# Three modulation vectors move from TensorE to VectorE, their weights turned by DMA, in a one-core transformer block

## The chip, the core and the metric

The kernel runs on one core of a Trainium2 chip. The metric is the device time of one execution in microseconds (us). A core has TensorE (matmuls, into PSUM), VectorE, ScalarE and GpSimd (POOL in the profile), each with an instruction queue of its own that it works through in order, and the SP engine, whose queue only issues DMA transfers here. POOL issues some transfers too. Engines wait for each other through semaphores; the scheduler of the kernel language sets those from the tiles that instructions read and write.

## The reference, cut to what matters

```python
mod = (silu(c) @ w_mod).reshape(1, 6, 1, 1024)          # c: [1, 1024], w_mod: [1024, 6*1024]
sa, ca, ga, sb, cb, gb = mod[:, 0] ... mod[:, 5]
h = layernorm(x) * (1 + ca) + sa                        # x: [1, 2048, 1024]
# linear attention, 32 heads of 32:
q, k, v = split(h @ wqkv);  phi(t) = where(t > 0, t + 1, exp(t)) + 1e-6
kv = einsum('bhsd,bhse->bhde', phi(k), v);  z = phi(k) summed over s
o = (phi(q) @ kv) / (phi(q) . z + 1e-6)
x = x + ga * (o @ wo)
h = layernorm(x) * (1 + cb) + sb
x = x + gb * ((silu(h @ w_gate) * (h @ w_up)) @ w_down) # w_gate, w_up: [1024, 3584]
```

All inputs are bf16. Each of the six modulation vectors is a product of one row, silu(c), with a 1024 x 1024 block of w_mod.

## The kernel before

The 2048 tokens are worked in four chunks of 512 (`sc` = 0 to 3), each of four tiles of 128. For each chunk the kernel computes phi(k) (`k_phase`, eight groups of eight 128x512 matmuls), adds the chunk before to the sum kv (`kv_phase`), and computes v (`v_phase`, eight groups). While v is computed, VectorE and ScalarE normalise the next chunk (`ln1`), a DMA transpose on the SP queue turns it to features by tokens (`hT`), and VectorE applies 1 + ca and sa (`modulate_all`). A phi group (`phi_to`) takes an exponential on ScalarE and two instructions on VectorE (L290, L292) before its PSUM buffer is free; `acc_a` has four such buffers, `acc_b` another four. V groups are evacuated by ScalarE alone.

phi(q) of chunk 0 follows its v; the Q groups of chunks 1 to 3 come after the last kv, as filling between small steps that wait for one another: `KVB` and `Zden` (VectorE, from the finished sum `kv_acc`), two TensorE transposes into `tpk` and their copy `KVT`, the sums of the denominator of chunk 0 (`den_sum(0)`), its reciprocal and its way through DRAM to a broadcast layout (`den_spread`), and four folds (`fold_wo`), which multiply kv into the output weight wo, so that attention and output projection become one product (`wo_tile`, matmul group a_ps). The four PSUM banks of a fold are emptied by ScalarE and VectorE, two each. Then come the second LayerNorm and the feed-forward part (`gate_up`, `down`), from about 210 us to the end.

The vectors sa and ca are computed at the start from `wma` and `wmb`; fillers (`keep_warm`, products of zeros) keep TensorE busy there. gb is summed on VectorE later (`gb_sum`, L366 and L368). The three others are made on TensorE: `ga_rows` in chunk 2 and `mod_rows` in chunk 3, between the fourth and the fifth K group, 32 narrow matmuls each into the tile `modr`, from blocks `wml` of w_mod that `mod_load` fetches on SP. The rows go through DRAM on the POOL queue: ga comes back as a broadcast `ga_bc`, sb and cb as columns `sbT` and `cb1T`. VectorE multiplies wo by `ga_bc` (L553) before the folds. Large tiles share one pool of 19 buffers (`big`).

TensorE's order is that of the program (`mm` keeps it). The order of the other engines is the scheduler's, except in the opening block `in_order` and where `tc.issue_after` names an instruction to follow. SP's queue is in order, so a transfer that waits for its buffer holds those behind it.

Of the kernel before, what the change touches and what calls it, by code (L numbers as in the profile page):

```python
# [15 lines left out]
LN_EPS = 1e-5  # L16
# [5 lines left out]
def kernel(  # L22
# [86 lines left out]
    def acc_b(name, shape=(NB,), dt=F32):  # L109
        return pb.tile([P] + list(shape), dt, name=name, tag="pb")  # L110
# [4 lines left out]

    x_tiles = {}

    def load_x(st, eng):
        x_sb = k2.tile([P, D], BF16, name="x_sb")
        eng.dma_start(out=x_sb[:], in_=x2[st * P:(st + 1) * P, :])  # L120
        x_tiles[st] = x_sb
# [64 lines left out]
    sa0T, ca0T = scr[:, :, 0, 0], scr[:, :, 1, 0]  # L186
    sbT = const.tile([P, DC], F32, name="sbT")
    cb1T = const.tile([P, DC], F32, name="cb1T")
    ga_t = ep.tile([P, NB], F32, name="e")
    ga_bc = ga_t[:].bitcast(BF16)  # L190
# [10 lines left out]
    def build_masks():  # L201
        nc.gpsimd.memset(zmask[:], 0.0)
        for h in range(HPC):
            rs = slice(h * DH, (h + 1) * DH)
            for hg in range(HG):
                nc.gpsimd.memset(zmask[rs, hg, HG * h + hg:HG * h + hg + 1], 1.0)

    def rstd_of(mv, n):
        veps = small.tile([P, STC], F32, name="veps")
        nc.vector.tensor_scalar_add(out=veps[:, 0:n], in0=mv[:, 0:n, 1], scalar1=LN_EPS)  # L210
        rstd = small.tile([P, STC], F32, name="rstd")
        nc.gpsimd.tensor_tensor(out=rstd[:, 0:n], in0=veps[:, 0:n], in1=neg_half[:].to_broadcast([P, n]), op=ALU.pow)  # L212
        return rstd
# [10 lines left out]
    def normalise_act(dst, src, mv, rstd):  # L224
        nmr = small.tile([P, 1], F32, name="nmr")
        nc.gpsimd.tensor_scalar(out=nmr[:], in0=mv[:, 0, 0:1], scalar1=rstd[:, 0:1], scalar2=-1.0,  # L226
                                op0=ALU.mult, op1=ALU.mult)
        nc.scalar.activation(out=dst, in_=src, func=ACT.Identity, bias=nmr[:], scale=rstd[:, 0:1])  # L228
# [20 lines left out]
    def ln1_norm(sc, t, x_sb, mv, rstd, dve=False):  # L249
        xn = k2.tile([P, D], BF16, name="xn", bufs=4)  # L250
        if dve:
            normalise(xn[:], x_sb[:], mv[:, 0, 0:1], rstd[:, 0:1])
        else:
            normalise_act(xn[:], x_sb[:], mv, rstd)
        if sc > 0:
            nc.sync.dma_start_transpose(hTs[sc][:, :, t * P:(t + 1) * P], xn[:])
        return xn
# [50 lines left out]
    def k_phase(sc, lo, hi):  # L308
        if lo == 0:
            pks[sc] = big("pk", [STC, D])  # L310
        for g in k_groups[lo:hi]:
            accs = [acc_a()]
            k_mms(sc, [g], accs)
            k_evac(sc, [g], accs)

    def v_phase(sc):
# [11 lines left out]

    def q_phase(sc, lo=0, hi=DC):
        if lo == 0:  # L330
            pqs[sc] = big("pq", [HG, SCW])
        for qc in range(lo, hi):
            acc = acc_a()
            for cc in range(DC):
                mm(acc[:], lhsT=wq[cc // 4][:, cc % 4, qc * P:(qc + 1) * P], rhs=hTs[sc][:, cc, :],
                                 start=(cc == 0), stop=(cc == DC - 1))
            phi_to(pqs[sc][:, qc, :], acc[:])

    def v_ones(v, lo):
# [3 lines left out]
    def kv_phase(sc):  # L343
# [7 lines left out]
        if sc == 0:  # L351
            nc.vector.tensor_copy(out=kv_acc, in_=kvv)
        else:
            nc.vector.tensor_tensor(out=kv_acc, in0=kv_acc, in1=kvv, op=ALU.add)

# [13 lines left out]

    def ga_rows(blks):  # L370
        ps = acc_b("modr")
        H2 = NB // 2
        for j in range(DC):
            for g in range(4):
                mm(ps[32 * g:32 * g + 32, 0:H2], lhsT=sc32[:, j, :], rhs=blks[g // 2][:, j, (g % 2) * H2:(g % 2 + 1) * H2],
                   start=(j == 0), stop=(j == DC - 1))
        row = small.tile([P, NB], BF16, name="mrow", bufs=1)
        nc.scalar.copy(out=row[:, 0:H2], in_=ps[:, 0:H2])
        for g in range(4):
            nc.gpsimd.dma_start(out=mrow_dram[0, g:g + 1, 0:H2], in_=row[32 * g:32 * g + 1, 0:H2])  # L380
        nc.gpsimd.dma_start(out=ga_bc.rearrange("p (g n) -> p g n", g=4),
                            in_=mrow_dram[0, :, 0:H2].unsqueeze(0).to_broadcast([P, 4, H2]))

    gb_rows = []

    def mod_load(cols):
        blks = []
        for lo in cols:
            t = big("wml", [DC, NB])
            nc.sync.dma_start(out=t[:], in_=wm_v[:, :, lo:lo + NB])  # L390
            blks.append(t)
        return blks

    def mod_rows(blks):
        ps = acc_b("modr")
        for j in range(DC):
            for g in range(4):
                mm(ps[32 * g:32 * g + 32, :], lhsT=sc32[:, j, :], rhs=blks[g][:, j, :],
                                 start=(j == 0), stop=(j == DC - 1))
        row = small.tile([P, NB], BF16, name="mrow", bufs=1)  # L400
        nc.scalar.copy(out=row[:], in_=ps[:])
        return row

    mrow_dram = dram.tile([2, 4, NB], BF16, name="mrow_scratch")

    def mod_spread(k, row):
        for g in range(4):
            nc.gpsimd.dma_start(out=mrow_dram[k, g:g + 1, :], in_=row[32 * g:32 * g + 1, :])
        cols = small.tile([P, 2 * DC], BF16, name="mcol", bufs=1)
        with nc.allow_non_contiguous_dma(reason="2048 elements, once"):  # L410
            nc.gpsimd.dma_start(out=cols[:], in_=mrow_dram[1].rearrange("g (i p) -> p (g i)", p=P))
        nc.vector.tensor_copy(out=sbT[:], in_=cols[:, 0:DC])
        nc.vector.tensor_scalar_add(out=cb1T[:], in0=cols[:, DC:2 * DC], scalar1=1.0)

# [9 lines left out]

    def den_sum(sc):
        pq = pqs[sc]
        den = acc_b("den")
        for hg in range(HG):
# [28 lines left out]
    def keep_warm(acc, n):  # L457
        for _ in range(n):
            mm(acc[:], lhsT=sel[:, 0, :], rhs=sel[:], start=True, stop=True)

    gs = k_groups[0:6]
    accs = [acc_a() if i < 4 else acc_b("acc") for i in range(6)]
    spare = accs[5]
    keep_warm(spare, 9)
    hT = hTs[0] = big("hT", [DC, SCW])
    pks[0] = big("pk", [STC, D])
    H = 3 * P
    with in_order(nc.vector, nc.scalar, nc.gpsimd):
# [8 lines left out]
        xns = [ln1_norm(*st0)] + [ln1_norm(*ln1_stats(0, t)) for t in range(1, 3)]  # L477
        keep_warm(spare, 6)
        mod_rows_a(0)
        pe_transpose_tile(hT, xns[0], 0)  # L480
        keep_warm(spare, 3)
        mod_rows_a(1)
# [31 lines left out]
    with tc.issue_after(last_on[nc.gpsimd.engine]):  # L514
        build_masks()
        nc.gpsimd.tensor_copy(out=scf[:], in_=scT[:])

    for sc in range(NSC):
        if sc > 0:
            k_phase(sc, 0, 2)  # L520
            kv_phase(sc - 1)
            k_phase(sc, 2, 4)
            if sc == 2:
                ga_rows(blks)
            if sc == 3:
                mod_spread(1, mod_rows(blks))
            k_phase(sc, 4, 8)
            if sc == 1:
                blks = mod_load([2 * D, 2 * D + NB])
            if sc == 2:  # L530
                blks = mod_load([3 * D, 3 * D + NB, 4 * D, 4 * D + NB])
        v_phase(sc)
# [3 lines left out]
        if sc == 0:  # L536
            q_phase(0, 0, 6)
        if sc + 1 < NSC:
            with tc.issue_after(last_phi[0].ins):
                modulate_all(hTs[sc + 1], ca1T, saT)  # L540
        if sc == 0:
            q_phase(0, 6, 8)
        if sc + 2 < NSC:
            for st in range((sc + 2) * STC, (sc + 3) * STC):
                load_x(st, nc.sync)
        if sc == 2:
            wo = [big("wo", [4, D]) for _ in range(2)]
            for h in range(2):
                for g in range(4):
                    nc.sync.dma_start(out=wo[h][g * DH:(g + 1) * DH, :, :], in_=wo_v[h, g])  # L550
            for cc in range(DC):
                w = wo[cc // 4][:, cc % 4, :]
                nc.vector.tensor_tensor(out=w, in0=w, in1=ga_bc, op=ALU.mult)  # L553

    q_phase(1, 0, 2)
    kv_phase(NSC - 1)
    nc.vector.tensor_copy(out=KVB, in_=kv_acc[:, :, 0:DH])
    nc.vector.tensor_tensor(out=Zden[:], in0=kv_acc[:, :, DH:DH + 1].to_broadcast([P, HG, DH]),
                            in1=zmask[:], op=ALU.mult)
    q_phase(1, 2, 4)  # L560
    tpk = acc_b("tp", (2, P), BF16)
    for h in range(2):
        transpose(tpk[:, h, :], KVB[:, 4 * h:4 * h + 4, :].rearrange("p g e -> p (g e)"))
    nc.vector.tensor_copy(out=KVT, in_=tpk[:])
    den_sum(0)
    den_spread(0)

    def fold_wo(h, nb):
# [7 lines left out]
        for g in range(4):  # L576
            (nc.scalar.copy if g % 2 == 0 else nc.vector.tensor_copy)(out=wo[h][:, g, ns], in_=ps[g][:])  # L577

    q_phase(1, 4, 6)
    fold_wo(0, 0)  # L580
    q_phase(1, 6, 8)
    fold_wo(0, 1)
    q_phase(2, 0, 2)
    fold_wo(1, 0)
    q_phase(2, 2, 3)
    fold_wo(1, 1)

# [92 lines left out]
    for st in range(STC):  # L680
        wo_tile(st)
    q_phase(2, 6, 8)
    q_phase(3, 0, 5)
    with tc.issue_after(last_phi[0].ins):
# [64 lines left out]
```

## Time and profile before

| what | value |
|---|---|
| median of 6 runs | 836.27 us (836.14 to 836.73) |
| the profiled execution | 836.32 us, of which its span 834.5 us |
| TensorE busy | 823.4 us, 99% of the span |
| VectorE, ScalarE, POOL busy | 317.5, 168.6, 67.5 us |
| DMA | 129.07 MB, mean 155 GB/s |
| modr matmuls | 32 of 128x256, 32 of 128x512 |
| granted TensorE clock | 1.00 |

The span runs from the first to the last recorded instruction. A row of the profile names line, engine, operation, output and inputs, the count, the busy time and the mean of one in ns, then the idle time ahead of it and what ended it. "PE" is TensorE, "PEld" its weight loads, "DVE" VectorE, "ACT" ScalarE. The chain that ended last is followed back from the last instruction, at each step to what released it; "issue" in it is time in which the engine waited for nothing that the profile shows.

### The profile page before, as it was taken

To read this page: it belongs to the slowest core of one execution; us is meant where nothing else is said; L and a number is where in the kernel's file an instruction comes from. 1 tells how busy PE (TensorE), PEld (TensorE's weight loads), DVE (VectorE), ACT (ScalarE), POOL (GpSimd) and SP (SyncE) were. 2 spreads that over 40 slices of the span, in tenths; PEclk is the share of its full clock that TensorE was granted. 3 is DMA by queue.
4 is the path that set the end of the run, shared out by engine and by line. 5 is a ranking of instruction groups with operands and counts; after the bars stand their busy time and mean duration, and the time that the engine had idled before them with its cause. 6 is when DMAs were issued, how large, how long until landed. Compare 5 with 4: busy or idle time off the path is not lost.

```text
span 834.5 us, 11191 instructions
## 1 busy us (share of the span) xinstructions
PE 823.4 (99%) x4560; PEld 378.6 (45%) x4641; DVE 317.5 (38%) x606; ACT 168.6 (20%) x253; POOL 67.5 (8%) x168
## 2 busy tenths in 40 slices
PE   8999999999999999999999999999999999999998
PEld 3444444444444444444444444444444444444444
DVE  5755643587344335522222244211114431111122
ACT  3445443334211111101111110111110101111000
POOL 2101201111130201100000010000001100000000
PEclk9999999999999999999999999999999999999999
DMA  9873790129998544636434183662505529710011
GB/s 326 292 202 90 227 191 1 34 64 293 350 257 259 190 150 143 186 123 212 145 113 140 44 227 95 220 221 81 172 1 158 160 69 331 238 54 1 17 59 51
DMA packets 125748, 129.07 MB, mean 155 GB/s; under 512 B 34112, under 2 KB 106304, under 8 KB 125184
## 3 DMA queue, kind: packets, MB, share of 16 engines
q1 hardware_dynamic: 121440, 114.97, 45.7%
q0 software_dynamic: 3968, 12.99, 5.2%
q8 instruction: 36, 0.59, 0.3%
q10 hardware_dynamic: 288, 0.40, 0.1%
q14 instruction: 16, 0.13, 0.0%
HBM read 108.27 MB, written 12.72 MB: 145 GB/s over the span
## 4 chain that ended last, share of the span: by engine, by line
PE 98%; DVE 1%; issue 1%; ACT 0%; POOL 0%
PE acc L98 90%; PE a_ps L98 7%; PE kvp L98 1%; PE modr L98 0%; DVE stats L218 0%; PE mod_ps L98 0%; PE den L98 0%; ACT xn L228 0%; DVE wo L577 0%; PE tp L101 0%; PE wf L98 0%; DVE pq L292 0%; ACT eb L289 0%; POOL rstd L212 0%; DVE mv L219 0%
## 5 line engine op out<-in xcount | busy, mean ns | idle before, releaser
L98 PE MATMUL acc<-h2T,wgu 128*128 128x512 bf16 x1756 | 385.7, 379 | 1.9
L98 PEld LDWEIGHTS <-wgu 128*128 128x128 bf16 x1792 | 175.3, 98 | 211.3
L98 PE MATMUL acc<-wd,gu 128*128 128x512 bf16 (+2 forms) x908 | 195.2, 372 | 0.9
L646 DVE TENSOR_TENSOR gu<-acc,e 128x512 bf16<-128x512 f32 x112 | 77.5, 692 | 289.8 <-PE acc L98 276.0
L645 ACT ACTIVATE e<-acc 128x512 f32<-128x512 f32 x112 | 66.9, 597 | 374.8 <-PE acc L98 363.4
L98 PEld LDWEIGHTS <-gu 128*128 128x128 bf16 x924 | 89.4, 98 | 104.4
L98 PEld LDWEIGHTS <-hT 128*128 128x128 bf16 x512 | 49.5, 98 | 59.6 <-issue 0.6
L667 DVE TENSOR_TENSOR e<-acc,gb_bc 128x512 f32<-128x512 f32 (+2 forms) x33 | 22.3, 676 | 131.5 <-PE acc L98 122.5
L98 PE MATMUL a_ps<-wo,pq 128*128 128x512 bf16 x250 | 56.9, 379 | 0.3
L98 PE MATMUL acc<-wk,hT 128*128 128x512 bf16 x248 | 56.3, 379 | 0.6 <-issue 0.3
L98 PE MATMUL acc<-hT,wq 128*128 128x512 bf16 x247 | 55.6, 379 | 0.9 <-issue 0.6
L98 PE MATMUL acc<-wv,hT 128*128 128x512 bf16 x251 | 55.6, 379 | 0.3
L289 ACT ACTIVATE eb<-acc 128x512 bf16<-128x512 f32 x64 | 37.8, 596 | 74.1 <-PE acc L98 70.9
L228 ACT ACTIVATE xn<-x,nmr,rstd 128x1024 bf16<-128x1024 f32 x16 | 19.8, 1241 | 126.2 <-POOL nmr L226 126.2
L614 POOL DMA_DIRECT2D x_scratch<-x x16 | 9.9, 616 | 377.5 <-DVE x L607 377.5
L98 PEld LDWEIGHTS <-pq 128*128 128x128 bf16 x256 | 25.0, 98 | 30.2
L98 PEld LDWEIGHTS <-wq 128*128 128x128 bf16 x256 | 24.6, 98 | 29.8 <-issue 0.9
L290 DVE TENSOR_SCALAR eb<-eb 128x512 bf16<-128x512 bf16 x64 | 18.5, 293 | 48.5 <-ACT eb L289 48.4
L607 DVE TENSOR_TENSOR x<-a_ps,x_sb 128x512 f32<-128x512 f32 x32 | 22.1, 692 | 7.8 <-PE a_ps L98 7.0
L212 POOL TENSOR_TENSOR rstd<-veps,neg_half 128x1 f32<-128x1 f32 x32 | 17.9, 560 | 80.6 <-DVE veps L210 70.9
L327 ACT CAST v<-acc 128x512 bf16<-128x512 f32 x32 | 18.2, 583 | 22.7 <-PE acc L98 22.1
L670 DVE TENSOR_TENSOR ob<-e,x1r 128x512 bf16<-128x512 f32 (+2 forms) x33 | 22.3, 676 | 1.0
(82 smaller groups left out, 274.7 us busy)
## 6 DMA issues: line engine op xcount, KB each, us to landing
wgu<-in_B_w_gate_dram SPq DMA_DIRECT2D x28, 1024.0 KB, 7.7
wgu<-in_B_w_up_dram SPq DMA_DIRECT2D x28, 1024.0 KB, 9.4
x_sb<-in_A_x_dram SPq DMA_DIRECT2D x32, 256.0 KB, 7.2
x_scratch<-x POOLq DMA_DIRECT2D x16, 512.0 KB, 3.1
x1r<-x_scratch SPq DMA_DIRECT2D x31, 256.0 KB, 2.9
wd<-in_B_w_down_dram SPq DMA_DIRECT2D x7, 1024.0 KB, 7.1
wml<-in_w_mod_dram SPq DMA_DIRECT2D x6, 1024.0 KB, 8.6
rbc<-rden_scratch POOLq DMA_DIRECT2D x16, 256.0 KB, 8.4
```

The lines of the kernel that those rows point to most:

```text
L98: return tc.keep_in_program_order(nc.tensor.matmul(out, lhsT=lhsT, rhs=rhs, start=start, stop=stop))
L212: nc.gpsimd.tensor_tensor(out=rstd[:, 0:n], in0=veps[:, 0:n], in1=neg_half[:].to_broadcast([P, n]), op=ALU.pow)
L228: nc.scalar.activation(out=dst, in_=src, func=ACT.Identity, bias=nmr[:], scale=rstd[:, 0:1])
L289: nc.scalar.activation(out=e[:], in_=acc, func=ACT.Exp)
L290: nc.vector.tensor_scalar(out=e[:], in0=e[:], scalar1=1.0, scalar2=PHI_EPS, op0=ALU.min, op1=ALU.add)
L327: nc.scalar.copy(out=v[:, t * D + nb * NB:t * D + (nb + 1) * NB], in_=acc[:])
L607: nc.vector.tensor_tensor(out=x1[:, ns], in0=a_ps[:], in1=x_t[:, ns], op=ALU.add)
L614: nc.gpsimd.dma_start(out=x1_dram[st * P:(st + 1) * P, :], in_=x1[:])
L645: nc.scalar.activation(out=sg[:], in_=ps[0][:], func=ACT.Silu)
L646: gm = nc.vector.tensor_tensor(out=guT[sc][f // GPT][:, f % GPT, :], in0=ps[1][:], in1=sg[:], op=ALU.mult)
L667: nc.vector.tensor_tensor(out=yt, in0=y_ps, in1=gb_bc[:, ns], op=ALU.mult)
L670: nc.vector.tensor_tensor(out=ob, in0=yt, in1=x1r, op=ALU.add)
```

## The change

The rows of w_mod for ga, sb and cb are now fetched by DMA transposes (`mod_load`, SP): two of 1024 x 512 for each vector, ga's at the end of chunk 0, sb's at the end of chunk 1, cb's at the end of chunk 2. A transposed tile `wmt` has output features on partitions and the 1024 inputs along the row, so VectorE makes 128 elements of a vector with one instruction (`mod_step`): rows times `sc_row` (silu(c) on every partition), with the sum along the row written to a column of `gaT`, `sbT` or `cbT`. There are 24 such steps: 4 in the V phase of chunk 1, 2 in the K phase and 4 in the V phase of chunk 2, 5 in the K phase and 7 in the V phase of chunk 3, and 2 behind the next Q group. `modr` and its ways through DRAM are gone.

`sc_row` is made in the opening by eight 128x128 products and two ScalarE copies, in place of three fillers; other fillers become float32 products. ga's columns are turned on VectorE and written to DRAM as 32 runs of 32 elements by four POOL transfers, then read back as the broadcast (`ga_spread`). The loads of wo move behind cb's transposes in SP's queue, and its multiplication by `ga_bc` behind the seven steps in the V phase of chunk 3. The transposes for `KVT` come one Q group earlier in TensorE's order; `den_sum(0)` takes a buffer of the other pool and stands directly ahead of the first fold; every fold has two Q groups ahead of the next.

```diff
     def mod_load(q, cols):
+        for h in range(2):
+            t = big("wmt", [DC // 2, D])
+            lo = q * D + h * NB
+            last = nc.sync.dma_start_transpose(t[:], w_mod[:, lo:lo + NB])
+            mod_steps.extend((t[:, i, :], cols[:, 4 * h + i:4 * h + i + 1]) for i in range(DC // 2))
+        return last
...
+        with tc.issue_after(anchor or last_phi[0].ins):
+            for _ in range(n):
+                rows, col = mod_steps.pop(0)
+                last = nc.vector.scalar_tensor_tensor(out=rows, in0=rows, scalar=scale, in1=sc_row[:], op0=ALU.mult,
+                                               op1=ALU.mult, accum_out=col)
...
+    K_STEPS = [(), (), (0, 2), (0, 2, 4, 5, 6)]
+    V_STEPS = [0, 4, 4, 7]
+
+    def ga_spread():
+        turned = small.tile([P, P], F32, name="dsum", bufs=1)
+        nc.vector.transpose(out=turned[:, 0:DH], in_=gaT[:])
+        row = small.tile([P, P], BF16, name="rb", bufs=4)
+        nc.vector.tensor_copy(out=row[:, 0:DH], in_=turned[:, 0:DH])
+        cells = ga_dram[0].rearrange("(i g r) -> g i r", g=4, r=DH)
         for g in range(4):
+            nc.gpsimd.dma_start(out=cells[g], in_=row[g * DH:g * DH + DC, 0:DH])
+        nc.gpsimd.dma_start(out=ga_bc, in_=ga_dram[:].to_broadcast([P, D]))
...
+    def keep_warm_f32(acc, n):
+        zeros = sel[:].rearrange("p h n -> p (h n)").bitcast(F32)
+        for _ in range(n):
+            mm(acc[:, 0:zeros.shape[1]], lhsT=zeros[:, 0:P], rhs=zeros, start=True, stop=True)
...
-    keep_warm(spare, 9)
+    keep_warm_f32(spare, 3)
+    keep_warm(spare, 2)
...
-        keep_warm(spare, 6)
+        keep_warm_f32(spare, 3)
         mod_rows_a(0)
         pe_transpose_tile(hT, xns[0], 0)
-        keep_warm(spare, 3)
+        for h in range(2):
+            for j in range(DC // 2):
+                mm(accs[h][:, j * P:(j + 1) * P], lhsT=scT[:, 4 * h + j:4 * h + j + 1].to_broadcast([P, P]), rhs=ident[:],
+                   start=True, stop=True)
+            nc.scalar.copy(out=sc_row[:, h * NB:(h + 1) * NB], in_=accs[h][:])
...
             kv_phase(sc - 1)
-            k_phase(sc, 2, 4)
-            if sc == 2:
-                ga_rows(blks)
-            if sc == 3:
-                mod_spread(1, mod_rows(blks))
-            k_phase(sc, 4, 8)
...
+            if sc == NSC - 1:
+                wo = [big("wo", [4, D]) for _ in range(2)]
+                for h in range(2):
+                    for g in range(4):
+                        with tc.issue_after(last_load[0].ins):
+                            nc.sync.dma_start(out=wo[h][g * DH:(g + 1) * DH, :, :], in_=wo_v[h, g])
+            k_phase(sc, 2, 8)
...
+        steps = mod_step(V_STEPS[sc], last_veps[0].ins if sc + 1 < NSC else None)
+        if sc == NSC - 1:
+            with tc.issue_after(steps.ins):
+                for cc in range(DC):
+                    w = wo[cc // 4][:, cc % 4, :]
+                    nc.vector.tensor_tensor(out=w, in0=w, in1=ga_bc, op=ALU.mult)
...
+    q_phase(1, 0, 1, 2)
+    q_phase(1, 1, 2)
     kv_phase(NSC - 1)
...
+    q_phase(1, 2, 3)
+    tpk = acc_b("tp", (2, P), BF16)
...
+    q_phase(1, 3, 4)
+    den_sum(0, acc_a())
+    fold_wo(0, 0)
+    den_spread(0)
     q_phase(1, 4, 6)
-    fold_wo(0, 0)
+    fold_wo(0, 1)
     q_phase(1, 6, 8)
-    fold_wo(0, 1)
+    fold_wo(1, 0)
     q_phase(2, 0, 2)
-    fold_wo(1, 0)
+    fold_wo(1, 1)
     q_phase(2, 2, 3)
-    fold_wo(1, 1)
```

## The prediction

> **What bounds the kernel now.** I read the page first: busy shares, then the chain that ended last, then that chain in order of time, then the groups and the queues' timelines around the edited stages.
>
> ```profile
> PE 823.4 (99%) x4560; PEld 378.6 (45%) x4641; DVE 317.5 (38%) x606; ACT 168.6 (20%) x253; POOL 67.5 (8%) x168
> ...
> PE 98%; DVE 1%; issue 1%; ACT 0%; POOL 0%
> ```
>
> TensorE is the bound and it hardly ever waits. A gain must be matmul time taken off TensorE or one of its few holes closed; a loss must be a new hole. The chain in order of time shows both kinds of place:
>
> ```profile
> 95.35 0.99 PE modr L98 x32
> ...
> 125.33 1.84 PE modr L98 x32
> ...
> 156.27 0.56 PE den L98 x32
> 156.83 0.16 issue
> ...
> 168.27 0.61 ACT eb L289
> 168.90 0.30 DVE eb L290
> 169.23 0.69 DVE pq L292
> 169.92 1.21 DVE wo L577 x2
> 171.17 0.43 PE wf L98 x13
> ```
>
> The columns are start, length, what. The two modulation products (modr) lie on the chain with their full 0.99 and 1.84 us, nothing else runs on TensorE meanwhile. At 168.27 the chain leaves TensorE: the last fold (wf) waits for the evacuations of the fold before, because only one Q group lies between them. The rows that price what is added:
>
> ```profile
> L368 DVE SCALAR_TENSOR_TENSOR x<-x_sb,scf,x 128x1024 f32<-128x1024 bf16 x4 | 5.1, 1282 | 0.1
> ...
> L553 DVE TENSOR_TENSOR wo<-wo,e 128x1024 bf16<-128x1024 bf16 x8 | 5.0, 686 | 3.3 <-DMA wo<-in_A_wo_dram 3.3
> ```
>
> and where VectorE and the SP queue stand now in the stages that receive the work (timelines, start and length):
>
> ```profile
> 136.64 0.69 DVE L292 SCALAR_TENSOR_TENSOR pk<-acc,eb 128x512 bf16<-128x512 f32 x1
> 150.38 0.30 DVE L290 TENSOR_SCALAR eb<-eb 128x512 bf16<-128x512 bf16 x1 [13.05 <-ACT eb L289]
> ...
> 153.50 0.29 DVE L557 CAST kvs<-kvs 128x256 bf16<-128x256 f32 x1
> ```
>
> ```profile
> 104.02 5.52 SPq L256 DMA_TRANSPOSE hT<-xn  x3
> 109.59 4.98 SPq L550 DMA_DIRECT2D wo<-in_A_wo_dram  x7
> ```
>
> VectorE idles 13.05 us through the last V phase. That is the hole the change fills, and KVB (the cast at 153.50) is the first thing TensorE needs from it afterwards.
>
> **The change, part by part.**
>
> *Removed from TensorE.* Both modr products: 0.99 + 1.84 = 2.83 us, all on the chain. With them go two ScalarE copies (0.37 and 0.59 us), ten POOL DMAs, and two tiny VectorE copies, none on the chain: nothing.
>
> *Folds and first denominator.* The fold at 168 us now has two Q groups (16 matmuls, 3.4 us) before each next fold. In the trace the last fold runs from 170.36 to 171.60, 1.24 us, where the others take 0.36 to 0.43: 0.80 us back. den and the first fold now stand together, so one of the 0.16 us gaps after a narrow product ("issue") goes. Sum 0.96 us.
>
> *Added to VectorE: 24 steps, S us each.* No row shows a scalar_tensor_tensor with bf16 output from SBUF and a column sum. The nearest is L368, same length, 1282 ns; an independent instruction behind it starts 1.19 us after it (239.98 to 241.17, the second of two in a row beginning 1.33 after 238.65). I add 0.06 us for writing the sum, what a VectorE instruction on one column takes of the queue (veps at 99.59, next start 99.66). S = 1.25. Below: two elements a cycle as in L553, 0.60 + 0.05 = 0.65. The Trainium skill [...]the Vector Engine (DVE) Microarchitecture Reference, "Performance modes — why throughput varies by op and dtype", lists copy, cast, tensor_scalar and tensor_tensor as enabled and not this instruction. L368 had a float32 operand and can't decide. I take the row. Above: full durations without overlap, 1.28 + 0.15 (veps' duration) = 1.43.
>
> Where they lie: 10 steps by the end of the third V phase, beside the LayerNorm statistics. VectorE's last statistics then end near 107 us (now 105.3), four steps later it is at 112, and its modulation of hT waits for the transposed xn until about then anyway (now 111.73); it needs 2.7 us and the next K phase starts at 116.0 (now 117.0). Hidden, with about 1 us to spare at the first chunk, and TensorE eats the chunks slower than they come.
>
> The other 14 are the price. I walk both engines on the clock of this trace, minus the 0.99 us already gained. TensorE: a group of 8 matmuls takes 1.726 us; K phase 4 runs from 116.0, with kv 1.15 + 0.16 inside and no modr, to 131.1; V phase to 144.9; two Q groups, kv with its gap, a third Q group: 151.4. There the transposes (tp) want KVB, one Q group earlier in the order than now. VectorE: an evacuation takes 0.94 us (0.33 + 0.61 between starts), so with a step after groups 4, 5 and 6 it needs 2.2 us a group where TensorE needs 1.73; it is through with the last K group at 134.3 (the fourth step of this phase still just covered). Seven steps, 8.75 us: 142.9. Eight multiplications of wo, which used to lie in K phase 4, 8 x 0.60: 147.8. Q group 1: 148.7. Two steps: 151.2. Q group 2: 152.2. kv addition 0.35, KVB 0.22, and 0.1 to be seen: 152.9. TensorE waits 1.5 us. What is late behind that: Zden (0.33 us after KVB) and KVT come before the third Q group ends, so den isn't held again; the accumulators are four, and the group that waits longest for its evacuation (the first Q group, 146.7 to 148.7) still frees its buffer in time. The same walk over the kernel as it is ends at 176.5, where the trace shows a_ps at 176.7, and finds its hole at the last fold, 0.77 us.
>
> *Moved DMAs.* SP issues six transposes of 1 MB in place of six plain loads; wo's eight loads now stand behind the last two, and three x loads ahead of them. The xn transposes are the only row: 256 KB in 5.52 / 3 = 1.84 us when they follow each other, so 7.4 us a MB. From below a plain 1 MB load (8.6 us issue to landing, several at once); above there is no row for a transpose that reads HBM. DMA: Bandwidth & Descriptors, "Latency and other measured facts", gives 261 GB/s for a transpose, an estimate of 4.0 us a MB; the row decides, and with either the first pair (from 49 us, wanted at 78) and the second (from 82, wanted at 109) are hidden. The third goes from 109.6 to 124.3, wo's first half is issued by 126.8 and lands by 136.6 at the slowest landing shown (9.8 us); wanted at 142.9. Hidden, 6 us to spare. The gate's way out through DRAM (POOL, 5 DMAs from 112 us) is wanted at the same 142.9: 1.6 and 4.8 us to landing by the rows of mrow now. Hidden.
>
> *The start.* Fillers become three float32 products of 256 columns and two of bf16 for nine bf16. TensorE is at half speed there: nine take 1.21 to 5.23 us. By the rule of four passes for true float32 (FP8 and Floating Point Precision, "TensorE Precision Notes") three take 2.56 us and two 0.85, an estimate: done near 4.7, the c product half a microsecond earlier. Behind it the fourth row product at 14.11 waited for w_mod (PEld 0.42 us on DMA wme), so at most 0.3 of that comes through; reloaded weights in each pass could cost 0.5 instead. I take 0 and keep both ends. The eight products and two copies for sc_row (0.6 us each on ScalarE at 11.9, idle till 27.7) take the room of three fillers: nothing.
>
> Sum: 2.83 + 0.96 - 1.5 = 2.3 us. The profiled execution took 836.32 us around a span of 834.5, the median of six is 836.27, the same; so 834.0 from the median. Some 0.2% (1.7 us) is what a measurement of this kernel can tell from no change.
>
> **The rivals.**
>
> *Late transposes (slower).* If a 1 MB transpose out of HBM takes T, wo's first half lands at 109.6 + 2T + 2.5 + 9.8. It meets VectorE's 142.9 at T = 10.5; from there every microsecond of T costs two on the path, for VectorE has no slack left. T = 11.65 eats the gain, T = 12.5 is slower by 0.2%, T = 14 gives 841. Against: the transposes shown need 7.4. For: those read SBUF, these fetch rows 12 KB apart. 14%.
>
> *Costlier steps (no change).* Between S = 1.22 and 1.5 twelve steps stand in line, so 0.01 us of S costs 0.12. At 1.43 the gain is 0.1 us: 836.1; at 1.5 it is a loss of 0.7. 16%.
>
> *Cheap steps.* At S = 0.65 VectorE is never late, 2.83 + 0.96 = 3.8: 832.5. 10%.
>
> *The change not doing what it says*: the order of instructions leaves no modr on TensorE; excluded.
>
> **The numbers.** The main case has 60%: S from 1.14 to 1.3 gives gains of 2.85 to 1.7, with the start 3.2 to 1.2, so 833.1 to 835.1; a tenth of it falls within 0.2%. Faster: 0.53 + 0.10 = 0.63. Same: 0.07 + 0.10 of the costlier steps + 0.03 = 0.20. Slower: 0.17. The range takes in cheap steps and the costlier ones, and the first part of late transposes: 832.4 to 837.2.
>
> **What would show it.** Right: no modr, first group of K phase 4 near 116.0, wo multiplied from about 142.9, a hole of 1 to 2 us before tp with KVB as its releaser, none at the last fold, a_ps near 174.4. Wrong: steps off 1.25 us; VectorE waiting for wmt or wo (late transposes); hT late at 116; a K phase 1 that starts off 15.4.

## The result, and the profile after

| kernel | median us | runs | profiled execution (span) us |
|---|---|---|---|
| before | 836.31 (835.82 to 836.73) | 36 | 836.32 (834.5) |
| changed | 834.2 (833.07 to 834.84) | 18 | 834.46 (832.6) |

The ratio is 0.9973, 95% interval 0.9967 to 0.9979: 2.1 us faster, where 2.3 was forecast. The main steps of the sum were right. A loss of 1.45 us that it did not have is nearly made up by a smaller hole at tp and by gains in the opening and at modr; that these nearly cancel is chance.

The page of the changed kernel, busy times and the shares of the chain that ended last:

```profile
PE 819.7 (98%) x4502; PEld 378.8 (45%) x4581; DVE 344.8 (41%) x655; ACT 168.9 (20%) x253; POOL 64.3 (8%) x166
...
PE 95%; DVE 3%; issue 1%; ACT 0%; POOL 0%; DVEq 0%
```

TensorE is still the bound, but VectorE now has 3% of the chain instead of 1%. The chain in order of time (start, length, what) shows where:

```profile
120.49 1.24 PE acc L98 x5
121.73 1.11 issue
122.84 4.07 PE acc L98 x18
126.94 0.61 ACT eb L295
...
139.30 3.52 DVE wmt L404 x7
142.82 4.83 DVE wo L557 x8
147.66 0.61 ACT eb L295
148.29 0.31 DVE eb L296
148.62 0.69 DVE pq L298
149.31 2.29 DVE wmt L404 x4
...
152.89 0.30 DVE kvs L576
153.24 0.28 PE tp L101 x2
...
167.59 0.36 PE wf L98 x16
...
174.96 7.77 PE a_ps L98 x36
```

No modr is left, and the last fold (167.59) no longer waits. From 126.94 the chain runs through the steps and wo's multiplication to KVB (152.89) and to the transposes tp: that is the forecast. The 1.11 us at 121.73, in which TensorE waits for nothing that the profile shows, is not.

The groups that answer to the rows that priced the steps:

```profile
L404 DVE SCALAR_TENSOR_TENSOR wmt<-wmt,sc_row 128x1024 bf16<-128x1024 bf16 x16 | 19.0, 1218 | 0.0
...
L557 DVE TENSOR_TENSOR wo<-wo,e 128x1024 bf16<-128x1024 bf16 x8 | 4.9, 687 | 0.0
...
L404 DVE DVE_READ_ACCUMULATOR wmt<-wmt,sc_row 128x1 f32 x16 | 1.3, 84 | 0.0
```

A step is two instructions, 1218 and 84 ns, and the second of them is overlapped by the next step: seven steps start 1.145 us apart (134.72 to 142.73). The double rate of the wo row, 687 ns for the same length, did not come. On the SP queue (timeline):

```profile
109.23 1.24 SPq L262 DMA_TRANSPOSE hT<-xn  x1
110.52 9.09 SPq L388 DMA_TRANSPOSE wmt<-in_w_mod_dram  x2
119.70 4.98 SPq L544 DMA_DIRECT2D wo<-in_A_wo_dram  x8
```

Two transposes of 1 MB take 9.09 us to issue, and the list of DMA issues gives a median of 7.5 us from issue to landing. VectorE never waits for wmt or wo.

TensorE by stages, in us, from the first start of each product in the profiles (KV 2 stands for the KV products of chunk 2, which lie in the K phase of chunk 3):

| from, to | before | changed | difference |
|---|---|---|---|
| 0 to first K matmul | 15.43 | 14.86 | -0.57 |
| first K matmul to KV 0 | 46.25 | 46.26 | 0.01 |
| KV 0 to KV 1 | 28.89 | 28.88 | -0.01 |
| KV 1 to KV 2 (first modr) | 29.97 | 28.95 | -1.02 |
| KV 2 to KV 3 (second modr) | 30.84 | 30.33 | -0.51 |
| KV 3 to a_ps (tp, den, folds) | 25.34 | 25.52 | 0.18 |
| a_ps to the end of the span | 657.8 | 657.8 | 0.0 |

The second modr took 1.84 us and gave only 0.51. The folds were to give 0.96, and the stage is longer. The experiments take these rows apart; all their times below are medians, and stages are from their profiles, one execution each. The kernel before, run beside each, had medians of 836.3 to 836.34.

One kind of "issue" in these profiles is no time at all. Behind narrow products the timelines show gaps of 0.16 us, and in each such profile some 80 matmul records are missing (before: 4560 matmuls for 4641 weight loads). Where none is missing (4613 of each in three kernels below, 4737 in a fourth) no gap of 0.16 appears, and the stages are as long: KV 2 to KV 3 takes 28.88 us with such a gap (half the shift, below) and without (split products). Such a gap is a matmul without its record.

### The profile page after: what moved, and what is told of

Same layout as the page of the kernel before. It is cut to its first block, busy times and chain, and to the rows that moved or that the text cites. A ratio compares the mean times of both kernels' runs of the same rounds, so it can differ in the third digit from the quotient of the medians.

```text
span 832.6 us, 11105 instructions
## 1 busy us (share of the span) xinstructions
PE 819.7 (98%) x4502; PEld 378.8 (45%) x4581; DVE 344.8 (41%) x655; ACT 168.9 (20%) x253; POOL 64.3 (8%) x166
## 4 chain that ended last, share of the span: by engine, by line
PE 95%; DVE 3%; issue 1%; ACT 0%; POOL 0%; DVEq 0%
PE acc L98 87%; PE a_ps L98 7%; DVE wmt L404 1%; DVE wo L557 1%; PE kvp L98 0%; DVE pk L298 0%; DVE stats L224 0%; PE mod_ps L98 0%; DVE eb L296 0%; PE wf L98 0%; PE den L98 0%; PE tp L101 0%; DVE pq L298 0%; ACT xn L234 0%; ACT eb L295 0%
## 5 line engine op out<-in xcount | busy, mean ns | idle before, releaser
L295 ACT ACTIVATE eb<-acc 128x512 bf16<-128x512 f32 x64 | 37.9, 596 | 76.1 <-PE acc L98 72.9
L627 DVE BATCH_NORM_STATS2 stats<-x 128x6 f32<-128x512 f32 x32 | 22.2, 694 | 1.1
```

The lines of the kernel that those rows point to most:

```text
L295: nc.scalar.activation(out=e[:], in_=acc, func=ACT.Exp)
L627: nc.vector.bn_stats(out=stats[:, nb, :], in_=x1[:, ns])
```

## The experiments

**Only the order of the folds.** The kernel before with the first denominator beside the first fold, tp one Q group earlier, and two Q groups ahead of every fold; modr stays.

```diff
-    q_phase(1, 2, 4)
...
-    den_sum(0)
-    den_spread(0)
...
+    q_phase(1, 2, 3)
...
+    q_phase(1, 3, 4)
+    den_sum(0, acc_a())
+    fold_wo(0, 0)
+    den_spread(0)
     q_phase(1, 4, 6)
-    fold_wo(0, 0)
+    fold_wo(0, 1)
...
```

> The kernel before with nothing of the change but the order of the denominator and the folds: the transposes for KVT one Q group earlier, den_sum(0) in a buffer of the other pool directly ahead of the first fold, two Q groups between the folds; modr stays on TensorE. Theory A (the hole at the last fold is 0.80 us and one narrow gap of 0.16 us goes): 0.8 to 1.0 us faster than before, 835.4, no hole at the transposes because VectorE isn't late there. Theory B (the hole at the last fold only moves to another place of the chain): 836.3, with a new hole between 152 and 176 us.

It took 835.44, ratio 0.9991 (0.9983 to 1.0), and KV 3 to a_ps 24.44 us where before has 25.34: 0.90 us, against 0.96 forecast. Its timeline on TensorE has no idle time ahead of tp or of a fold:

```profile
154.23 0.28 PE L101 MATMUL tp<-ident,kvs 128*128 128x128 bf16 x2
...
156.73 0.43 PE L98 MATMUL wf<-wo,kvs 32*32 32x512 bf16 x16
...
168.50 0.43 PE L98 MATMUL wf<-wo,kvs 32*32 32x512 bf16 x16
```

So the earlier tp costs nothing here, where VectorE is not behind.

**tp after the fourth Q group.** The changed kernel with KVB's transposes where they were.

```diff
-    q_phase(1, 2, 3)
+    q_phase(1, 2, 4)
...
-    q_phase(1, 3, 4)
```

> The changed kernel with the two transposes for KVT behind the fourth Q group of chunk 1, as before, in place of the third; all else as changed. Theory A (VectorE comes to KVB about 1 us too late for the third group and has time enough for the fourth): no TensorE idle time at the transposes (0.91 us in the changed kernel), KVT ready before the denominator sums end, 0.7 to 0.9 us faster, 833.4. Theory B (the lateness isn't lost at the transposes alone; the fold waits for KVT instead): the same time, with the hole at the first fold.

It took 833.1, ratio 0.9961 (0.9948 to 0.9973), 1.1 us below the changed kernel. The same place on TensorE, first in the changed kernel:

```profile
153.24 0.28 PE L101 MATMUL tp<-ident,kvs 128*128 128x128 bf16 x2 [0.91 <-DVE kvs L576]
...
155.19 0.63 PE L98 MATMUL acc<-pq,Zden 128*32 128x128 bf16 x32
155.75 0.43 PE L98 MATMUL wf<-wo,kvs 32*32 32x512 bf16 x16
```

and with the later tp:

```profile
154.07 0.28 PE L101 MATMUL tp<-ident,kvs 128*128 128x128 bf16 x2
154.27 0.63 PE L98 MATMUL acc<-pq,Zden 128*32 128x128 bf16 x32
154.87 0.44 PE L98 MATMUL wf<-wo,kvs 32*32 32x512 bf16 x16
```

The bracket is the idle time and its releaser, KVB on VectorE. One Q group of cover removes it, and neither den nor the fold waits in exchange. KV 3 to a_ps falls from 25.52 to 24.48: the hole is worth 1.04 us.

**The opening.** The changed kernel with its first fillers as before.

```diff
-    keep_warm_f32(spare, 3)
-    keep_warm(spare, 2)
+    keep_warm(spare, 9)
```

> The changed kernel with the nine bf16 fillers of before at the very start, in place of three float32 and two bf16 ones; all else as changed. Theory A (the first K product starts 0.57 us earlier in the changed kernel because the c product is released earlier and the whole opening chain follows it): the c product goes back from 4.79 to about 5.2 us, the first K matmul from 14.86 to about 15.4 us, and the kernel loses 0.4 to 0.6 us (834.7). Theory B (the opening is bound by the loads of w_mod, as the prediction took it; the 0.57 us come from the products and copies for sc_row taking the room of three fillers): the first K matmul stays near 14.9 us and the time at 834.2.

It took 834.52, ratio 0.9977 (0.9968 to 0.9986), 0.3 above the changed kernel with overlapping intervals; the first K matmul started at 15.80. Alone this is weak: in that profile the first row product also waited 1.3 us for w_mod (0.65 in the changed kernel). A second, better pair stands at the end of this section.

**The hole at 121.7, first guess: the transposing loads.** Around it the DMA engines nearly stop. Windows of one microsecond in the changed kernel (the last two columns are the DMA share and GB/s):

```profile
120.00:121.00 1.00, 0.84 (x25) 0.61 (x21) 0.97 (x5) 0.00 (x0) 0.00 (x0) 1.00 2.80 233
121.00:122.00 1.00, 0.73 (x4) 0.12 (x2) 0.39 (x2) 0.00 (x0) 0.00 (x0) 1.00 0.13 5
122.00:123.00 1.00, 0.16 (x1) 0.11 (x2) 0.00 (x0) 0.00 (x0) 0.00 (x0) 1.00 0.93 237
```

The guess was that cb's transposes do this. They alone became plain loads of the same size; these bring other elements, so cb is not the vector that it should be.

```diff
-            last = nc.sync.dma_start_transpose(t[:], w_mod[:, lo:lo + NB])
+            last = nc.sync.dma_start(out=t[:], in_=wm_v[:, 4 * h:4 * h + 4, q * D:(q + 1) * D])
```

> The changed kernel with the two DMA transposes for cb turned into two plain loads of as many bytes (so cb holds wrong sums; nothing else is left out). Theory A (TensorE's 1.1 us without work at 121.7 us, in the fourth K phase, comes from DMA: its next block of instructions, fetched by DMA, is held up by the transposes in flight): no such hole, the fetch of 16 KB that the changed kernel got at 120.3 us comes near 112 us, 0.7 to 1.1 us faster, 833.3, and the spread over runs is as narrow as before (0.6 us in place of 1.8). Theory B (the hole comes from where the 256-instruction blocks end in the dense kv products): hole and time stay. Theory C (the hole is VectorE's steps holding an accumulator): hole and time stay, too, but the row names VectorE.

The guess that the transposes make the hole fell. The kernel took 835.93 (835.3 to 839.07), 1.7 us above the changed kernel, and in the profiled execution, the slowest of its runs, the hole had grown:

```profile
120.25 1.24 PE L98 MATMUL acc<-wk,hT 128*128 128x512 bf16 x5 [0.16 <-issue]
124.67 12.10 PE L98 MATMUL acc<-wk,hT 128*128 128x512 bf16 x42 [3.18 <-issue]
```

while its plain loads went on without a pause (the column ahead of the DMA share is the granted clock):

```profile
121.00:122.00 1.00, 0.49 (x3) 0.00 (x0) 0.30 (x1) 0.00 (x0) 0.00 (x0) 1.00 1.14 219
122.00:123.00 1.00, 0.00 (x0) 0.00 (x0) 0.00 (x0) 0.00 (x0) 0.00 (x0) 1.00 0.99 201
123.00:124.00 1.00, 0.00 (x0) 0.00 (x0) 0.00 (x0) 0.00 (x0) 0.00 (x0) 0.84 1.10 225
```

Only a part of the loss is the hole: inside it, at 123.67, the granted clock fell to 0.50 and stayed there until 130.50, so the same 42 recorded matmuls took 12.10 us where they take 9.24 behind the hole of the changed kernel.

**Second guess: TensorE's own instructions.** The page lists a DMA queue of the kind "instruction", 36 packets and 0.59 MB, 16,384 bytes each. In the trace's DMA records these packets fall one for about every 255 TensorE instructions (4581 weight loads, each with its matmul, for 36 packets; 37 packets for 4737 in the realigned kernel below). The Trainium skill (Runtime: NRT & Kernel Launch, "Instruction fetch mechanics") says the same: instructions are streamed in 16 KiB blocks of 256, at a cost "mostly hidden". The size and the count agree with the trace; "hidden" is what is in question here. The 128 narrow KV products with their weight loads are 256 instructions in 1.15 us, a whole block. In the changed kernel one such packet starts at 120.30 and takes 1.14 us; TensorE runs dry at 121.73 and goes on at 122.84. With plain loads the packet starts at 121.80 and TensorE goes on at 124.67.

Without modr the KV products follow each other at exactly 512 instructions, so all of them stand at the same place of a block. The test moves that place without changing a column of work: 32 products of Q phase 1 (phi(q) of chunk 0, ahead of all KV products) in two halves, which are 64 more instructions.

```diff
+            w = SCW // 2 if sc == 0 and qc < 4 else SCW
-            for cc in range(DC):
-                mm(acc[:], ..., rhs=hTs[sc][:, cc, :], ...)
+            for o in range(0, SCW, w):
+                for cc in range(DC):
+                    mm(acc[:, o:o + w], ..., rhs=hTs[sc][:, cc, o:o + w], ...)
```

> The changed kernel with 32 products of Q phase 1 (its first four groups) each multiplied in two halves of 256 columns: 64 more TensorE instructions and the same columns, all ahead of the first KV products. Theory A (TensorE runs out of instructions at 121.7 us because the KV products of chunk 2 eat one whole block of 256 instructions in 1.4 us just when a block begins, and the next block comes late): with every block boundary moved by 64 instructions off the KV products, the 1.1 us hole marked 'issue' in K phase 4 is gone, a_ps starts near 173.7 and the median is 833.1. Rival B (the hole is the DMA engines' doing at that place, wherever the blocks begin): the hole stays at some 1.1 us, median 834.2. Under both the 32 further products may add up to 0.2 us.

833.63, ratio 0.9968 (0.9957 to 0.998). The hole is gone: KV 2 to KV 3 takes 28.88 us, down from 30.33, and TensorE, with every matmul recorded, has no "issue" wait in its table of waits. But 0.5 us was lost in the stage before, KV 1 to KV 2: 29.47 us, up from 28.95. TensorE's weight loads and VectorE show why (two timelines):

```profile
116.16 0.10 PEld L98 LDWEIGHTS <-hT 128*128 128x128 bf16 x1 [0.18 <-DVE hT L237]
116.48 0.10 PEld L98 LDWEIGHTS <-hT 128*128 128x128 bf16 x1 [0.23 <-DVE hT L237]
```

```profile
114.97 0.41 DVE L237 TENSOR_SCALAR hT<-hT,sca 128x512 bf16<-128x512 bf16 x1 [1.92 <-DMA hT<-xn]
```

hT of chunk 3 came later (VectorE could start on it at 113.47 in the changed kernel), and TensorE took each piece of it as VectorE finished it. In this kernel an instruction packet starts at 109.83, among hT's transposing loads, and they stop:

```profile
109.00:110.00 1.00, 1.00 (x6) 0.47 (x5) 1.00 (x3) 1.00 (x3) 0.00 (x0) 1.00 1.18 225
110.00:111.00 1.00, 1.00 (x7) 0.47 (x5) 1.00 (x3) 0.40 (x2) 0.00 (x0) 1.00 2.04 43
111.00:112.00 1.00, 1.00 (x7) 0.41 (x6) 1.00 (x3) 0.49 (x1) 0.00 (x0) 1.00 0.50 149
```

On the SP queue the last of hT's loads takes 2.22 us to issue, where it takes 1.24 in the changed kernel (109.23):

```profile
109.71 2.22 SPq L262 DMA_TRANSPOSE hT<-xn  x1
```

That is the standstill of 121 us again. It goes with a fetch among transposing loads: in the five kernels whose packet falls on wmt's transposes here (at 120.3 to 120.9, 118.8 and 115.7 us) they stop too, in the last of these (half the shift, below) without any wait on TensorE. So it is what a fetch does to transposing loads, not what keeps TensorE waiting.

**Both edits.** The changed kernel with the split products and the later tp.

> Both edits together: the split products of Q phase 1, and KVB's two transposes after the fourth Q group and not after the third. Theory A: the two holes (1.1 us 'issue' in K phase 4, 0.9 us ahead of tp) lie on the same chain and add: median 832.1, a_ps from 173.0. Rival B (the hole of K phase 4 stays): 833.1, as with the later transposes alone.

832.76, ratio 0.996 (0.9948 to 0.9973). KV 2 to KV 3 28.88 and KV 3 to a_ps 24.48: the two gains add. KV 1 to KV 2 is again 29.47, so the forecast of 832.1 was missed by the late hT.

**The modulation vectors alone.** The split products, the new steps, and den, tp and folds in the old order.

```diff
+    q_phase(1, 2, 4)
...
+    den_sum(0, acc_b("den"))
+    den_spread(0)
...
-    q_phase(1, 2, 3)
...
-    q_phase(1, 3, 4)
-    den_sum(0, acc_a())
+    q_phase(1, 4, 6)
     fold_wo(0, 0)
-    den_spread(0)
-    q_phase(1, 4, 6)
+    q_phase(1, 6, 8)
     fold_wo(0, 1)
...
```

> The changed kernel with the split products of Q phase 1 and with the first denominators and the folds in the old order (tp after the fourth Q group, then den, the first fold two Q groups later). It leaves the modulation vectors' move as the only part. Theory A (moving the modulation vectors off TensorE is worth the 2.8 us of the modr matmuls plus 0.3 to 0.6 at the start; the new order of the folds is worth 0.9 and its earlier tp gives 0.9 back): median 833.1, equal to the changed kernel with the split products within 0.2, no hole at tp, narrow gap at the last fold back. Rival (the sum's own sizes: the folds worth 0.96, the hole at tp 1.5): this kernel 0.5 faster than the changed kernel with the split products.

833.4, ratio 0.9965 (0.9953 to 0.9978), 0.2 below the kernel with the split products and the new order. KV 3 to a_ps is 25.35 here and 25.52 there: the new order gives 0.9 and its earlier tp takes 1.04, so this part of the change, as it was made, is worth nothing. All of the gain comes from the move of the vectors, with the opening that belongs to it. The late hT cost less here: a packet starts at 110.29 and the last of hT's loads takes 2.05 us to issue, but KV 1 to KV 2 takes 29.07 us, 0.2 above the 28.88 of an undisturbed stage and not 0.6.

**The kernel before, realigned.** 96 of its products in halves, so that the KV products of chunk 2 stand in a block about where they stand in the changed kernel. Its loads here are plain.

> The kernel before with 96 more TensorE instruction pairs and the same columns (all of Q phase 1 and half the groups of K phase 2 multiplied in halves of 256 columns), so that the KV products of chunk 2 stand at the same place in the 256-instruction blocks as in the changed kernel; no transposing loads here, plain loads in flight at that time. Theory A (the place in the block decides): a hole of about 1 us marked 'issue' appears in K phase 4 some 1.2 us after those products, and the median is 837.4. Rival A2 (the place in the block matters only with transposing loads in flight): no hole, 836.3. Under both the 96 further products may add up to 0.5 us.

839.03, ratio 1.0032 (1.002 to 1.0044), 2.7 us slower; 0.5 of that are the halves themselves. A hole of the expected size did appear, but not where the theory had it: it came in the first modr, which starts 4.7 us behind the start of the KV products of chunk 1.

```profile
95.81 0.94 PE L98 MATMUL modr<-wml,sc 128*32 128x256 bf16 x27
97.94 0.39 PE L98 MATMUL modr<-wml,sc 128*32 128x256 bf16 x5 [1.18 <-issue]
```

An instruction packet starts at 95.32. The 64 instructions of modr are the dense stretch here, and no transposing load is in flight. Behind the KV products of chunk 2, where the hole was expected, there is a small one: two K matmuls start 0.53 us apart (125.65 and 126.17) in place of 0.22, a loss of 0.31 us. So a change of instruction count alone makes such a hole, with plain loads too, but the KV products are not the only place, and the size is not given by the place alone.

**Half the shift, and the opening again.** If the packet must fall neither on hT's transposes (up to 112 us) nor behind the KV products (119), half as many split products should do. The later tp is kept (`qc < 2` for `qc < 4`).

> The changed kernel with KVB's transposes after the fourth Q group and only 16 products of Q phase 1 in halves (two groups, 32 more TensorE instructions, half as many as in the two kernels of the last call). Theory A2 (an instruction fetch that falls among transposing loads stops those loads for about 1 us; with 64 more instructions it fell at 110 us, on the transposes of chunk 3's hT, which then came 1 us late and cost 0.5 us in K phase 4; with 32 more it falls some 3.5 us later, behind hT's transposes and still ahead of the KV products of chunk 2): neither the 1.1 us hole in K phase 4 nor the wait of the weight loads for DVE hT is there, from the KV products of chunk 1 to those of chunk 2 it is 28.9 us and from chunk 2 to 3 again 28.9, median 832.3 (0.5 below the last kernel of the last call). Rival (the lateness of hT has nothing to do with the fetch): the wait for hT stays, from chunk 1 to 2 it is 29.5 us, median 832.8.

832.33 (832.3 to 832.6), ratio 0.9953 (0.9941 to 0.9966), faster than before by 4.0 us and than the changed kernel by 1.9. The packet starts at 115.69. The chain no longer leaves TensorE in these stages, and what is left of "issue" are the 0.16 us of a matmul without its record:

```profile
119.44 1.15 PE kvp L98 x128
120.59 0.16 issue
120.75 10.74 PE acc L98 x49
...
153.03 0.11 PE tp L101 x2
...
172.90 7.77 PE a_ps L98 x36
```

The last kernel is the same with the opening's fillers as before the change, and with one group of Q phase 1 in halves to keep the instruction count near.

> The kernel above with all warming products of the opening as in the kernel before (9 and 6 of bf16 128x512), one group of Q phase 1 in halves so that the KV products stand 8 instructions from where they stand above. Theory A (the float32 fillers let the first K matmul start earlier, by the mean of the profiles so far 0.3 us): 0.3 us above the kernel beside it, first K matmul near 15.4 to 15.5. Rival B (the opening is worth nothing, its differences are those of the first w_mod loads from run to run): equal within 0.1 us.

832.97, ratio 0.9961 (0.9947 to 0.9975), 0.64 above. Its first K matmul starts at 15.42, against 15.16: 0.26 us for the opening. The rest came from the instructions:

```profile
119.47 1.20 PE L98 MATMUL kvp<-v,pk 128*32 128x64 bf16 x125
120.94 0.21 PE L98 MATMUL kvp<-v,pk 128*32 128x64 bf16 x3 [0.27 <-issue]
```

The packet starts at 118.78, and TensorE runs dry three KV products short of the end.

In the trace a float32 product is two weight loads and two matmuls (six of each for three products), so the fillers count. With that, the place of the first KV product of chunk 2, as the number of TensorE instructions ahead of it modulo 256, and what followed. Every matmul has a weight load and none of those is missing, so the number is twice the weight loads recorded ahead.

| kernel | place | packet starts, relative to KV 2 | TensorE ran dry |
|---|---|---|---|
| before | 230 | -7.7 us | no |
| changed | 174 | +1.35 | at 186, 1.11 us |
| later tp | 174 | +1.3 | at 186, 1.16 us |
| plain loads for cb | 174 | +2.9 | at 186, 3.18 us |
| old first fillers | 176 | +1.05 | at 186, 1.14 us |
| old fillers, one group split | 192 | -0.7 | at 186, 0.27 us |
| half the shift | 206 | -3.7 | no |
| split products | 238 | -10.05 | no |

"Ran dry at" is the place, modulo 256, of the instruction that waited. In all five it is the one with 1978 TensorE instructions ahead of it: a K product in four kernels, a KV product in the fifth. In the realigned kernel the hole in modr comes out at 188 and the small one behind KV 2 at 186. It is always the same edge of a block.

The edge is where TensorE runs dry, but standing near it is not enough. In the changed kernel all four groups of KV products stand at 174, and only the third runs dry; the packets of the others start 0.9 us before, 0.1 us behind and 3.4 us before their first KV product. So the time of the packet decides with the place. The same count with plain loads in flight had its packet 1.5 us later than with transposes, so the loads may hold it up; no experiment here takes that apart.

## Why the prediction was right, point by point

| step of the sum | forecast us | measured us | from |
|---|---|---|---|
| modr off TensorE | -2.83 | -3.04 | KV 1 to 2 and KV 2 to 3: 29.97 and 30.84 to 28.89 and 28.88 (old fillers with one group split; split products) |
| folds and den | -0.96 | -0.90 | 25.34 to 24.44, folds alone |
| hole at tp | +1.5 | +1.04 | 25.52 to 24.48, later tp |
| the start | 0 | -0.57 here, -0.26 in the pair | first K matmul |
| instruction fetch | not there | +1.45 | KV 2 to KV 3, 30.33 where 28.88 is free of it |
| sum | -2.3 | -1.92, a_ps from 176.72 to 174.80 | |

The measured terms add up to -2.02; the other 0.1 is in stages that differ by some hundredths from profile to profile. The 1.45 is the profiled execution's: between the medians of the later tp and of half the shift, which differ by the split products alone, it is 0.77 (833.1 to 832.33), and 1.2 between their profiled executions.

*modr.* Right. The step into a narrow stretch went with it, twice: the first modr product starts 0.31 us behind the last K product (94.97 to 95.28, 124.95 to 125.26 before), where K products follow each other at 0.22.

*Folds.* Right at the last fold, 0.80 us. The 0.16 us that the sum took for a gap behind a narrow product was a matmul without its record; that leaves 0.1 us of the measured 0.90, about what one step into a narrow stretch costs, and den against the fold saves one.

*S.* 1.145 us, not 1.25, inside the stated 1.14 to 1.3. The row L368 was the right neighbour; the 0.06 us for writing the sum were too much, since the accumulator's read is overlapped by the next step. The twelve steps that stand in line also take their scalar as a constant; the eight beside the statistics read it from memory, as L368 does, and start 1.21 us apart, 1283 ns long. The double rate of the cheap-steps rival does not hold for this instruction as it is used here: 1218 ns, and 687 in the wo row beside it. The Trainium skill's list of enabled instructions that the prediction cites (Vector Engine (DVE) Microarchitecture Reference, "Performance modes — why throughput varies by op and dtype"), which leaves this one out, agrees. Whether it would hold without the column sum was not tried.

*The hole at tp.* Right in place, releaser and cause; 0.91 us where 1.5 was forecast. The seven steps took 8.01 us instead of 8.75, but 0.65 of that was not kept: VectorE then waited for the exponential of the first Q group (148.29, `[0.65 <-ACT eb L295]`). From that point two steps, 2.29 us, remain ahead of KVB. At this S only those two set the hole, so by an estimate from these figures S would have to be near 0.69 to close it, 0.91 / 2 less. The split products bear this out: without the loss at 121.7 us upstream they have the same 0.65 and the same 0.91. The prediction said that twelve steps stand in line from 1.22 up, and gave 2.85 us of gain for S = 1.14, which is a hole of 0.94. The walk was right, but for a slip of 0.15 us in it (134.3 and 8.75 make 143.05, not 142.9; its 147.8 goes with 143.05); the term S was mis-sized.

*The start.* The step "at most 0.3 of that comes through; I take 0" was too cautious. The estimate for the fillers held: the c product starts at 4.79 us, where near 4.7 was forecast, 0.37 earlier than before. In the pair 0.26 reached the first K matmul. Over seven profiles with all of the new opening the first K matmul starts at 14.84 to 15.37, over four with all of the old one at 15.39 to 15.43: the gain varies, and the profiled execution lies at its upper end.

*Transposes.* 7.4 us a MB was taken from the xn row; the pairs took 9.0 to 10.8 us to issue, 4.5 to 5.4 each, and wo was there when VectorE came at 142.73 (142.9 was forecast). The rival of late transposes had no ground. At 4.5 us the 4.0 estimated from the 261 GB/s of the Trainium skill (DMA: Bandwidth & Descriptors, "Latency and other measured facts") was nearer to the pace than the row of transposes from SBUF.

*What was not in the sum.* That TensorE can run out of instructions. The profile before held one sign, the instruction queue on its page; its gaps of 0.16 us marked "issue", one of which the prediction counted, are no sign of it. The missing 1.45 us on one side, and on the other the hole at tp (0.46 smaller) with the start and modr (0.78 more gain), largely cancel. Nothing in the prediction's working made them cancel: that the number came out within 0.2 us is in part luck.

What stays open is how far ahead a block is asked for, and what delays its packet. The packet of the same edge starts 10 us ahead of the KV products in one kernel and 3.7 in another, 32 instructions apart, and 32 K instructions take only 3.5 us. Whether the 3.18 us with plain loads is waiting behind their packets was not isolated. The small shifts were not tried with other loads in flight.

## What to carry to other kernels

When a change takes work off the bound engine and fills an idle one, find the first hand-over back: here one more Q group ahead of tp was worth 1.04 us, half the gain. Read every "issue" gap of the bound engine against the packets of its instruction queue, and first against the count of its records: weight loads and matmuls that do not match mean gaps that are none. Where narrow products use up a block in a microsecond, some matmuls in halves upstream can move the edge of the block off them, but look at what the fetch then falls on, above all transposing loads.

## What the runs showed of the hardware that was not expected

- TensorE waits for its instructions: 1.11 us in the changed kernel, 1.18 in the kernel before realigned, 3.18 with plain loads in flight; it goes on 1.2 to 1.5 us after the end of a packet that takes 1.0 to 1.4. A shift of some tens of instructions, with the same work, decides.
- An instruction packet among transposing loads stops them for more than a microsecond: 233 to 5 GB/s at 121 us of the changed kernel (42 or less in every quarter of a microsecond from 120.75 to 122.25), 225 to 43 at 110 us of the kernel with split products. Plain loads went on at 201 to 219.
- In the hole of 3.18 us the granted clock fell to 0.50, 2.2 us after TensorE ran dry, and stayed there for 6.8 us; in the hole of 1.11 us it stayed at 1.00.
- VectorE's scalar_tensor_tensor on bf16 from SBUF, with a column sum, takes 1218 ns for 1024 elements, 65 more with a scalar from memory; the column sum is an instruction of 84 ns, which the next step overlaps.
- A float32 product of 256 columns is two matmuls with two weight loads in the records.
- The step from products of 512 columns into a narrow stretch costs 0.09 us (0.31 us between starts in place of 0.22).
